# A float32 attention and FFN kernel: sign pass of the float64 weights on ScalarE, first products of two chunks interleaved, first tiles transposed by a diagonal

## The chip, the cores and the metric

The kernel runs on one core of one Trainium2 chip. The metric is the device time of one execution in microseconds (us). Before the change it took 611.33 us, the median of three runs (608.84 to 612.02).

## The reference

Four batches of 768 tokens with 8 heads of 64 go through a banded attention; each token then goes through a normalization and a two-layer network, whose weights are float64.

```
scores = scale * q @ k.T            # q, k, v: (4, 8, 768, 64) float32
keep = is_global | is_local         # first 8 keys, or 0 <= row - col < 96
scores = where(keep, scores - slope_h * dist, -1e9)
a = exp(scores - max(scores)); a = a / (sum(a) + 1e-9)
x = (a @ v) as (4, 768, 512)
xn = (x - mean(x)) / sqrt(var(x) + 1e-6) * g_ln
out = x + maximum(xn @ w_ch1, 0) @ w_ch2      # w_ch1 (512, 2048), w_ch2 (2048, 512), float64
```

## The kernel before

The 3072 tokens are 24 tiles of 128 rows; a chunk is two tiles (256 tokens), so there are twelve chunks. The first four tiles (t = 0 to 3, `TILES`) are the first 128 rows of each batch, for which one block of keys is enough; the program calls them `short`. They make up chunks 0 and 1. Their way is (names as in the trace): k and q are loaded (kf, qf) and transposed on TensorE (tk, tq), copied out of PSUM (kT, qT), multiplied to scores (s, two groups g of four heads). VectorE adds the mask and takes the negative maximum nm (T <- s, mask). ScalarE adds a constant to nm (mn) and takes the exponentials of each head with their sum (T <- T, mn). T is transposed on TensorE (tp), copied out (pT) and multiplied with v (pv). `divide` (L723) makes the reciprocal r of the sums and x = pv * r. Mean and variance follow, GpSimd raises to the power -0.5 (rs), `centred` writes (x - mean) * g into xs, `scaled` (L757) multiplies xs by rs, and `turn` (L450) transposes it on TensorE (tx). Two passes write it to xT as a sum of two f16 halves: high on ScalarE, low on VectorE. For the later tiles the transposes are DMAs, and their f16 low parts (pn, kn, xn, ul) are subtractions on GpSimd or VectorE.

All the big products are made of f16 halves. The weights are read as raw float64 and turned into an upper and a lower f16 by integer and float passes on 16 pieces of 128x1024 words (`weight`, L331 to 385). Pieces 0 to 7 are w1 (two per quarter of its columns, so steps 0 and 2 need pieces 0 and 1, steps 4 and 6 pieces 2 and 3, and so on), pieces 8 to 15 are w2. The passes of a piece n are, by their task names: wb, the load (1 MB); wr, `below` on ScalarE (bits below the mantissa); ws, `signs` on VectorE; wz, `sizes` on ScalarE (the float32 exponent rebased, absolute value); ww, `whole` on VectorE (shift and or); wu, the upper f16 (a cast, on whichever engine is chosen); wl, the lower f16 (a subtraction). In the trace the tile that they work on is st, or w2h or w2l where a piece has its home in the place of later weights. The sign pass before is

```
vec.tensor_scalar(out=halves[n][:, :, 1], in0=halves[n][:, :, 3],
                  scalar1=0x8000, scalar2=None, op0=ALU.bitwise_and)
```

A first product F{c}_{f} (`ffn1`, L809; f1_c_f in the order, f in the trace) takes xT of chunk c times two column blocks of w1: 24 matmuls of 128x256. Its result is evacuated as h in two f16 halves: a ReLU on ScalarE or VectorE, and a SCALAR_TENSOR_TENSOR on VectorE. The second products G (`ffn2`, L907) take h times w2. From the fifth chunk on, a scheme with seven products in place of eight takes over (R, uh, ul, m). None of this is touched by the change.

The order of the work comes from a planner (class `Plan`, L92 to 186). Each step is a task with an engine (or several, with a cost each), a cost in us, a rank, its predecessors and the buffers that it takes. A list scheduler gives each engine the task that can begin first; among those that can begin at about the same time, the lowest rank. A task with several engines goes to the one on which it would end first, with a handicap (`FAVOR` early, `LATER` later). The tables at the top (QUICK for the first tiles, PIECE and START for the weights) set the ranks. Gaps that the plan finds on TensorE before 90 us (`UNTIL`) are filled with `blank`, a product of the identity with itself (L264). Every instruction is issued through a helper (`Lane`), so all carry the line L204 in the trace. The first products are put in order by the loop at L1063 to 1090: all eight steps of chunk 0, then all eight of chunk 1, each after the one before it (`steps[-1:]`).

Of the kernel before, what the change touches and what calls it, by code (L numbers as in the profile page):

```python
# [24 lines left out]
P = 128  # L25
# [18 lines left out]
CT = 2  # L44
# [6 lines left out]

QUICK = (0.0, -5.2, 7.7, 16.9)
PIECE = (1.8, 5.3, 15.0)
START = 37.6
SIDE = (-1.1, 1.1)
UNTIL = 90.0


# [21 lines left out]
EVEN = 4  # L80
EARLY = 150.0
LEAD = 11
VRANK = 6.0
VLATE = 0.0
WEIGH = (-0.8, 0.2)
FAVOR = {"ACT": SIDE[0], "POOL": SIDE[1]}
# [103 lines left out]
def banded(ctx, tc, q, k, v, n_global, n_local, g_ln, w1, w2, out, flag):  # L190
# [37 lines left out]
    plan.room.update(ld=6, h=17, T=3, pn=3, pT=3, s=3, s1=1, pv=1, f1=2, f2=2, kT=3, vn=3, kT0=2, vn0=2, qT=2, r=2, tile=2, x=5, xT=2, st=3)  # L228
    task = plan.task
# [91 lines left out]
    for h in range(H):  # L321
        task(f"mask1_{h}", {"POOL": 0.87, "ACT": 0.42, "DVE": 0.3}, 0, lambda engine, h=h: build_mask1(h, engine), ["globals"], rank=45, port=True)
    task("gb", "SP", 0.6, lambda: load.dma_start(out=gb, in_=g_ln.partition_broadcast(P)), rank=9, dma=0.7)
# [7 lines left out]
    def weight(n):  # L331
# [50 lines left out]
        task(f"wl{n}", {"POOL": 2.2, "DVE": 1.24}, 0, lower, [f"wu{n}"], rank=rank, port=True)  # L382

# [65 lines left out]

    def turn(src, name, tag):  # L450
        ps = ps_f.tile([P, 4, P], F32, tag=tag, name=name)
        last = None
        for u in range(4):
            last = chain(last, pe.transpose(ps[:, u, :], src[:, u * P:(u + 1) * P], ident))
        return ps
# [131 lines left out]
    def tile_(t, ranks, gates):  # L587
# [116 lines left out]
        for g in range(ng_):  # L704
# [4 lines left out]
            task(f"R{t}_{g}", "DVE", 0.85 if short else 0.95, lambda g=g: reduce(g), [f"S{t}_{g}"] + ([f"mask0_{h}" for h in heads(g)] if short else []), rank=rank - 3, take={"T": [f"tp{t}_{g}" if short else f"pl{t}_{g}"]})  # L709
            task(f"E{t}_{g}", "ACT", 1.7 if short else 1.5, lambda g=g: exps(g), [f"R{t}_{g}"], rank=rank - 3)  # L710
            if short:
# [11 lines left out]
    def normal(t, rank, last, short):  # L723

        def divide():
            x, _, _ = place_x(t)
            sm = smalls[t][2]
            if short:
                r = p2.tile([P, H], F32, name="r")
                vec.tensor_scalar(out=r, in0=sm, scalar1=PS * 1e-9, scalar2=1.0 if short else VS, op0=ALU.add, op1=ALU.mult)  # L730
            else:
                r = made.pop(("r", t))
            vec.reciprocal(out=r, in_=r)
            vec.tensor_tensor(out=x, in0=sums.pop(t), in1=r.unsqueeze(2).to_broadcast([P, H, D]), op=ALU.mult)

        def divisor():
            made["r", t] = p2.tile([P, H], F32, name="r")
            act.activation(out=made["r", t], in_=smalls[t][2], func=AF.Copy, scale=VS, bias=PS * 1e-9 * VS)

# [69 lines left out]
    def ffn1(c, f, rank):  # L809
# [97 lines left out]
    def ffn2(ts, f, n, tags, rank):  # L907
# [152 lines left out]
    def due(step):  # L1060
        return START + step * place_rank

    for t in range(2 * CT):  # L1063
        tile_(t, [QUICK[t]] * 2, [[], []])
    for c in range(NC):
        if c < 2:
            for f in range(0, NF, 2):
                ffn1(c, f, due(len(steps)))
            if c == 0:
                continue  # L1070
# [294 lines left out]
```

## Time and profile before

| | before |
|---|---|
| median of three runs | 611.33 us (608.84 to 612.02) |
| profiled execution | 610.96 us, its span 609.2 us |
| TensorE (PE) busy | 590.0 us, 97% |
| TensorE weight loads (PEld) | 487.8 us, 80% |
| VectorE (DVE) busy | 518.7 us, 85% |
| ScalarE (ACT) busy | 410.5 us, 67% |
| GpSimd (POOL) busy | 160.5 us, 26% |
| granted clock of TensorE | 0.99 and more in every slice |

The page divides the span into 40 slices of 15.2 us. PE is at 8 or 9 tenths from the first slice, but until 90 us that includes the blanks. DVE is at 9 tenths through most of the first third. The wait lists put the idle time of an engine down to what ended it; a matmul's end is modelled, so starts are better than durations on PE.

### The profile page before, as it was taken

How to read it: one execution, taken by the hardware profiler on the slowest of the kernel's cores; microseconds unless marked ns; L12 is line 12 of the kernel's file. 1: busy time of each engine (PE TensorE's matmuls, PEld its weight loads, DVE VectorE, ACT ScalarE, POOL GpSimd, SP SyncE). 2: the span in 40 equal slices, each digit the busy share in tenths (PEclk: the TensorE clock that was granted, in tenths of full speed). 3: DMA queues.
4: the chain of work that ended last, by engine and by line, in shares of the span. 5: the costliest groups of instructions: out<-in, count | busy, mean ns of one | idle time of the engine just before them, and what ended most of it. 6: DMA issues, size and time to landing. Idle time of an engine off the chain costs nothing.

```text
span 609.2 us, 15299 instructions
## 1 busy us (share of the span) xinstructions
PE 590.0 (97%) x5913; PEld 487.8 (80%) x5913; DVE 518.7 (85%) x1248; ACT 410.5 (67%) x1008; POOL 160.5 (26%) x128
## 2 busy tenths in 40 slices
PE   8979899999999999999999999999999999999996
PEld 4757696556965885789999999999999999988885
DVE  5999999999999988899789899898898788484654
ACT  5988797875677866778676666889866755333330
POOL 2210112405464227252032032152232031040100
PEclk9999999999999999999999999999999999999999
DMA  8992989987988996985949866878966625100000
GB/s 220 304 320 97 226 204 199 231 195 126 222 165 184 198 168 138 185 172 112 168 122 132 148 156 110 156 153 148 165 140 98 130 53 88 36 36 18 36 2 37
DMA packets 247307, 88.33 MB, mean 145 GB/s; under 512 B 237376, under 2 KB 237376, under 8 KB 247232
## 3 DMA queue, kind: packets, MB, share of 16 engines
q1 hardware_dynamic: 246944, 87.32, 68.6%
q8 instruction: 47, 0.77, 0.5%
q14 instruction: 28, 0.23, 0.1%
q10 hardware_dynamic: 288, 0.00, 0.0%
HBM read 38.01 MB, written 6.29 MB: 73 GB/s over the span
## 4 chain that ended last, share of the span: by engine, by line
PE 62%; DVE 4%; DMA 2%; issue 1%; ACT 0%; SPq 0%; DVEq 0%
PE f L204 31%; PE m L204 24%; PE s L204 4%; PE pv L204 3%; DMA out_dram<-x 1%; DMA qT<-qT 1%; DMA xT<-xn 1%; DVE x L204 1%; DVE pn L204 0%; DVE T L204 0%; DVE w2l L204 0%; DVE R L204 0%; DVE vn L204 0%; DVE qn L204 0%; DVE xn L204 0%
## 5 line engine op out<-in xcount | busy, mean ns | idle before, releaser
L204 PE MATMUL f<-xT,w1h 128*128 128x256 f16 x1536 | 256.5, 273 | 7.8 <-DVE h L204 3.2
L204 PE MATMUL f<-xT,w1l 128*128 128x256 f16 x768 | 209.3, 273 | 0.0
L204 PEld LDWEIGHTS <-w1h 128*128 128x128 f16 x1536 | 147.4, 98 | 25.2 <-DVE xT L204 2.5
L204 DVE SCALAR_TENSOR_TENSOR R<-f,R 128x128 f32<-128x128 f32 x256 | 68.3, 288 | 35.0 <-ACT R L204 29.7
L204 ACT ACTIVATE T<-T,mn 128x256 f32<-128x256 f32 (+1 forms) x192 | 92.5, 482 | 3.5
L204 PEld LDWEIGHTS <-uh 128*128 128x128 f16 x896 | 85.9, 98 | 9.4
L204 PEld LDWEIGHTS <-w1l 128*128 128x128 f16 x768 | 75.1, 98 | 9.5 <-issue 0.8
L204 PE MATMUL f<-w2h,h 128*128 128x512 f16 x256 | 80.4, 379 | 0.5 <-DVE h L204 0.5
L204 ACT ACTIVATE uh<-R 128x896 f16<-128x896 f32 x57 | 53.9, 946 | 39.1 <-DVE R L204 39.0
L204 DVE CUSTOM_DVE_ANT_0 T<-s,mask 128x256 f32<-128x256 f32 (+1 forms) x192 | 68.2, 396 | 11.0 <-PE s L204 10.9
L204 ACT ACTIVATE R<-f 128x512 f32<-128x512 f32 x59 | 35.0, 594 | 62.6 <-PE f L204 61.1
L204 PE MATMUL m<-w2h,uh 128*128 128x256 f16 x256 | 69.8, 273 | 0.0
L204 PE MATMUL m<-w2l,uh 128*128 128x256 f16 x256 | 69.8, 273 | 0.0
L204 PE MATMUL m<-w2h,ul 128*128 128x256 f16 x256 | 69.8, 273 | 0.0
L204 PE MATMUL m<-t,uh 128*128 128x256 f16 x384 | 69.5, 273 | 0.0
L204 PEld LDWEIGHTS <-h 128*128 128x128 f16 x384 | 36.3, 98 | 40.1 <-issue 0.8
L204 POOL TENSOR_TENSOR ul<-R,uh 128x896 f16<-128x896 f32 x17 | 32.4, 1905 | 121.4 <-ACT uh L204 121.4
L204 DVE TENSOR_TENSOR ul<-R,uh 128x896 f16<-128x896 f32 x47 | 54.1, 1150 | 12.1 <-ACT uh L204 11.8
L204 POOL TENSOR_TENSOR pn<-T,pn 128x512 f16<-128x512 f32 x27 | 33.7, 1249 | 113.8 <-ACT pn L204 90.8
L204 PE MATMUL s<-kT,qT 128*128 128x128 f16 (+1 forms) x704 | 55.7, 225 | 2.0 <-ACT T L204 1.1
L204 PE MATMUL m<-t,ul 128*128 128x256 f16 x192 | 52.3, 273 | 0.0
L204 ACT ACTIVATE pn<-T 128x512 f16<-128x512 f32 x78 | 48.6, 623 | 2.3 <-DMA xT<-xn 0.9
(154 smaller groups left out, 1007.4 us busy)
## 6 DMA issues: line engine op xcount, KB each, us to landing
st<-in_moe_w_ch_dram SPq DMA_DIRECT2D x10, 1024.0 KB, 6.4
kf<-in_k_dram SPq DMA_DIRECT2D x28, 256.0 KB, 3.8
vf<-in_v_dram SPq DMA_DIRECT2D x28, 256.0 KB, 3.9
qf<-in_q_dram SPq DMA_DIRECT2D x24, 256.0 KB, 3.7
out_dram<-x SPq DMA_DIRECT2D x24, 256.0 KB, 2.6
qT<-qT SPq DMA_DIRECT2D x40, 128.0 KB, 2.6
w2h<-in_moe_w_ch_dram SPq DMA_DIRECT2D x3, 1024.0 KB, 7.7
w2l<-in_moe_w_ch_dram SPq DMA_DIRECT2D x3, 1024.0 KB, 9.6
```

The lines of the kernel that those rows point to most:

```text
L204: ins = getattr(self.engine, name)(*args, **kw)
```

## The change

It has five parts. (1) The sign pass may run on ScalarE too: there it reads the upper 32-bit word of the float64 as a float32, multiplies it by 2^-100 and writes an f16, which is a zero with the word's sign. (2) For the four first tiles the scaling of xs by rs is gone; instead the identity times rs (a 128x128 diagonal) is the right-hand operand of a float32 product that transposes xs and scales it at once. (3) The constant is no longer added to nm for these tiles; the divisor r takes an adjusted constant and is made on ScalarE. (4) The steps F of chunks 0 and 1 are put in order by MIX, and each waits for the step before it of its own chunk only. (5) All rank tables and several costs have new numbers, so the planner writes another order.

```
-QUICK = (0.0, -5.2, 7.7, 16.9)
-PIECE = (1.8, 5.3, 15.0)
-START = 37.6
+QUICK = (0.0, -57.0, 17.4, 26.0)
+PIECE = (24.7, 9.6, 9.5)
+START = 54.9
...
+MIX = [(0, n) for n in range(4)] + [(c, n + 4 * (1 - c)) for n in range(4) for c in (1, 0)] + [(1, n) for n in range(4, 8)]
...
-        def signs():
+        def signs(engine):
+            if engine == "ACT":
+                act.activation(out=halves[n][:, :, 1].bitcast(F16), in_=staged[n][1].bitcast(F32), func=AF.Copy, scale=2.0 ** -100)
+                return
             vec.tensor_scalar(out=halves[n][:, :, 1], in0=halves[n][:, :, 3], scalar1=0x8000, scalar2=None, op0=ALU.bitwise_and)
...
-        task(f"ws{n}", "DVE", 0.7, signs, [f"wr{n}"], rank=rank, port=True)
+        task(f"ws{n}", {"ACT": 1.24, "DVE": 1.34}, 0, signs, [f"wr{n}"], rank=rank, port=True)
...
-    def turn(src, name, tag):
+    def turn(src, name, tag, by=None):
...
+            if by is not None:
+                last = chain(last, pe.matmul(ps[:, u, :], lhsT=src[:, u * P:(u + 1) * P], rhs=by, start=True, stop=True))
+            else:
+                last = chain(last, pe.transpose(ps[:, u, :], src[:, u * P:(u + 1) * P], ident))
...
-            act.activation(out=mn[:, gsl], in_=nm[:, gsl], func=AF.Copy, bias=LN_PS)
+            if short:
+                mn = nm
+            else:
+                gsl = slice(g * gh, (g + 1) * gh)
+                act.activation(out=mn[:, gsl], in_=nm[:, gsl], func=AF.Copy, bias=LN_PS)
...
-        def scaled(engine):
-            xc = made["xc", t]
-            copy(engine, xc, xc, made["rs", t])
+        def diagonal(engine):
+            if engine == "ACT":
+                act.activation(out=made["diag"][t % 3], in_=ident, func=AF.Copy, scale=made["rs", t])
+            else:
+                vec.tensor_scalar(out=made["diag"][t % 3], in0=ident, scalar1=made["rs", t], scalar2=None, op0=ALU.mult)
...
-            made["xt", t] = turn(made["xc", t], f"tx{t}", "f1" if t < 2 else "f2")
+            made["xt", t] = turn(made["xc", t], f"tx{t}", "f1" if t < 2 else "f2", made["diag"][t % 3])
...
-        after = [...] + steps[-1:]
+        after = [...] + ([f"F{c}_{f - 2}"] * (f > 0) if c < 2 else steps[-1:])
```

The first place is ScalarE ahead of the last copy into xT0, which holds chunk 0 for its first product (T is a tile of exponentials, w2l the home of weight pieces 2 and 3 at that time; "less" marks the pass `below`, "big" the pass `sizes`, and w2l<-w2l alone is a sign pass). Before:

```order
L204 ACTIVATE xs0_424<-xs0_424,rs_359 128x512
L204 ACTIVATE xs1_407<-xs1_407,rs_397 128x512
L204 ACTIVATE mn_417<-nm_416 128x4
L204 ACTIVATE T2_0_434,sm_418<-T2_0_434,mn_417 128x128 x4
L204 ACTIVATE xT0_333<-tx1_460 128x4x128
L204 ACTIVATE xT0_333<-tx0_449 128x4x128
```

And now:

```order
L207 ACTIVATE T3_1_494,sm_442<-T3_1_494,nm_440 128x128 x4
L207 ACTIVATE r_519<-sm_442 128x8
L207 ACTIVATE xT1_424<-tx2_508 128x4x128
L207 ACTIVATE pT3_0_526<-tp3_0_514 128x512
L207 ACTIVATE w2l_86<-w2l_86,less_93 128x1024
L207 ACTIVATE pT3_1_549<-tp3_1_534 128x512
L207 ACTIVATE w2l_86<-w2l_86 128x1024
L207 ACTIVATE w2l_86,big_92<-w2l_86 128x1024
L207 ACTIVATE w2l_86<-w2l_86,less_93 128x1024
L207 ACTIVATE xT0_309<-tx0_562 128x4x128
```

The scalings of xs and the additions (mn) are gone; the exponentials of the last first tile, two weight pieces' passes and a copy into xT1 now stand ahead of the copy that fills xT0.

The second place is VectorE between the evacuations of the first products (h0_2 is step 2 of chunk 0, h1_0 step 0 of chunk 1; st4 to st6 are weight pieces). Before:

```order
L204 SCALAR_TENSOR_TENSOR st5_382<-st5_382 128x1024
L204 TENSOR_SCALAR st6_465<-st6_465 128x1024
L204 TENSOR_TENSOR xT1_589<-tx2_666,xT1_589 128x4x128
L204 SCALAR_TENSOR_TENSOR h0_2_615<-f1_0_2_564,h0_2_615 128x512
L204 TENSOR_TENSOR w1l_84<-st5_382,w1h_83 128x2x512
L204 TENSOR_SCALAR w2h_85<-w2h_85 128x1024
L204 SCALAR_TENSOR_TENSOR st6_465<-st6_465 128x1024
L204 SCALAR_TENSOR_TENSOR h0_4_741<-f1_0_4_629,h0_4_741 128x512
```

And now:

```order
L207 SCALAR_TENSOR_TENSOR h0_2_664<-f1_0_2_634,h0_2_664 128x512
L207 SCALAR_TENSOR_TENSOR st5_420<-st5_420 128x1024
L207 CAST w1h_83<-st5_420 128x2x512
L207 TENSOR_TENSOR w1l_84<-st5_420,w1h_83 128x2x512
L207 SCALAR_TENSOR_TENSOR st6_457<-st6_457 128x1024
L207 CAST w1h_83<-st6_457 128x2x512
L207 SCALAR_TENSOR_TENSOR h0_4_758<-f1_0_4_699,h0_4_758 128x512
L207 TENSOR_TENSOR w1l_84<-st6_457,w1h_83 128x2x512
L207 SCALAR_TENSOR_TENSOR h1_0_727<-f1_1_0_669,h1_0_727 128x512
L207 SCALAR_TENSOR_TENSOR h1_2_790<-f1_1_2_733,h1_2_790 128x512
```

The sign passes (TENSOR_SCALAR) have left this queue, the casts have come to it, and evacuations of chunk 1 stand between those of chunk 0.

## Rows read from the trace of the kernel before

**Rows 1.** Windows: stretch, us, busy (xinstructions) of PE PEld DVE ACT POOL, PEclk, DMA share, GB/s

```profile
0.00:39.00 39.00, 31.87 (x193) 20.83 (x193) 30.44 (x98) 30.80 (x88) 10.20 (x15) 1.00 0.90 269
39.00:70.00 31.00, 27.00 (x227) 22.53 (x228) 30.17 (x54) 25.21 (x50) 3.83 (x3) 1.00 0.64 200
70.00:100.00 30.00, 29.85 (x304) 26.60 (x303) 29.15 (x50) 27.22 (x56) 3.08 (x2) 1.00 0.92 199
100.00:250.00 150.00, 148.43 (x1361) 98.59 (x1360) 143.39 (x291) 106.30 (x281) 61.54 (x48) 1.00 0.92 182
```

**Rows 2.** PE's waits, 0 to 76 us: waited for, us in total, times, longest

```profile
PE f L204 <- DVE h L204: 3.2, 3, 1.9
PE f L204 <- ACT kT L204: 2.2, 1, 2.2
PE tx L204 <- ACT xs L204: 1.6, 1, 1.6
```

**Rows 3.** Timeline of PE: start, us, instruction, count, idle before and its releaser

```profile
39.24 0.28 PE L204 MATMUL f<-xT,w1h 128*128 128x256 f16 x1 [2.16 <-ACT kT L204]
...
69.92 0.38 PE L204 MATMUL f<-xT,w1h 128*128 128x256 f16 x2
...
72.54 0.60 PE L204 MATMUL tx<-ident,xs 128*128 128x128 f32 x4
72.97 0.38 PE L204 MATMUL f<-xT,w1h 128*128 128x256 f16 x2
```

**Rows 4.** Groups by form, weight passes: count, busy us, mean ns, idle before

```profile
L204 DVE TENSOR_SCALAR st<-st 128x1024 uint16<-128x1024 uint16 x10 | 13.0, 1346 | 0.0
L204 ACT ACTIVATE st<-st 128x1024 f32<-128x1024 f32 x10 | 11.5, 1147 | 0.2 <-DVE st L204 0.2
...
L204 ACT ACTIVATE w1h<-st 128x1024 f16<-128x1024 f32 x2 | 2.3, 1167 | 0.1
...
L204 DVE CAST w1h<-st 128x1024 f16<-128x1024 f32 x1 | 0.7, 686 | 0.0
```

**Rows 5.** Timeline of DVE up to the first product

```profile
10.15 0.29 DVE L204 CUSTOM_DVE_ANT_0 T<-s,mask 128x128 f32<-128x128 f32 x1 [1.12 <-PE s L204]
...
10.37 0.29 DVE L204 CUSTOM_DVE_ANT_0 T<-s,mask 128x128 f32<-128x128 f32 x1
...
20.68 1.23 DVE L204 TENSOR_TENSOR w1l<-w2h,w1h 128x1024 f16<-128x1024 f32 x1
21.82 0.17 DVE L204 TENSOR_SCALAR r<-sm 128x8 f32<-128x8 f32 x1
22.02 0.20 DVE L204 RECIPROCAL r<-r 128x8 f32<-128x8 f32 x1
...
24.08 1.35 DVE L204 TENSOR_SCALAR w2h<-w2h 128x1024 uint16<-128x1024 uint16 x1
25.21 1.40 DVE L204 TENSOR_SCALAR w2l<-w2l 128x1024 uint16<-128x1024 uint16 x1
...
38.51 1.28 DVE L204 TENSOR_TENSOR xT<-tx,xT 128x512 f16<-128x512 f32 x2
```

**Rows 6.** Timeline of ACT, one group of four exponentials

```profile
12.19 0.40 ACT L204 ACTIVATE T<-T,mn 128x128 f32<-128x128 f32 x1
...
13.74 0.57 ACT L204 ACTIVATE kT<-tk 128x512 f32<-128x512 f32 x1
```

**Rows 7.** Groups by form, the first tiles

```profile
L204 PE MATMUL s<-kT,qT 64*128 64x128 f32 x64 | 6.8, 284 | 1.5 <-ACT T L204 1.1 <-ACT qT L204 0.3
...
L204 ACT ACTIVATE xs<-xs,rs 128x512 f32<-128x512 f32 x4 | 2.8, 718 | 1.8 <-DVE xs L204 1.8
...
L204 ACT ACTIVATE mn<-nm 128x4 f32<-128x4 f32 x8 | 1.6, 195 | 0.0
```

**Rows 8.** Groups by form, low parts on POOL

```profile
L204 POOL TENSOR_TENSOR pn<-T,pn 128x512 f16<-128x512 f32 x27 | 33.7, 1249 | 113.8 <-ACT pn L204 90.8 <-DVE nm L204 12.1 <-issue 3.7
L204 POOL TENSOR_TENSOR ul<-R,uh 128x896 f16<-128x896 f32 x17 | 32.4, 1905 | 121.4 <-ACT uh L204 121.4
```

More of the change, by code (lines that the diff above doesn't have):

```diff
@@ L80 @@
 EVEN = 4
[L81 to L85, printed above, removed]
+EARLY = 153.0
+LEAD = 9
+VRANK = 14.4
+VLATE = 15.0
+WEIGH = (-1.4, -0.21)
 FAVOR = {"ACT": SIDE[0], "POOL": SIDE[1]}
@@ L227, in banded @@
     plan = Plan()
-    plan.room.update(ld=6, h=17, T=3, pn=3, pT=3, s=3, s1=1, pv=1, f1=2, f2=2, kT=3, vn=3, kT0=2, vn0=2, qT=2, r=2, tile=2, x=5, xT=2, st=3)
+    plan.room.update(ld=6, h=17, T=3, pn=3, pT=3, s=3, s1=1, pv=1, f1=2, f2=2, kT=3, vn=3, kT0=2, vn0=2, qT=2, r=2, tile=2, x=5, xT=2, st=3, dg=3)
     task = plan.task
@@ L262, in starts, with beside @@
         pool.memset(made["ones"], 1.0)
+    def beside():
+        made["aside"] = aside = p2.tile([P, 1024], F16, tag="pn", name="aside", bufs=3)
+        made["diag"] = [aside[:, 2 * P * n:2 * P * (n + 1)].bitcast(F32) for n in range(3)]
     def blank():
@@ L312, in banded @@
     task("ident", "DVE", 0.3, lambda: vec.tensor_scalar(out=ident, in0=made["rel"][:, 1, :], scalar1=0.0, scalar2=None, op0=ALU.is_equal), ["starts"])
+    task("beside", "DVE", 0.0, beside, ["ident"], rank=-4, take={"pn": [f"xt{2 * CT - 1}"]})
     task("asked", "ACT", 0.95, asked, rank=-50, dma=-4.7)
@@ L321, in banded @@
     for h in range(H):
-        task(f"mask1_{h}", {"POOL": 0.87, "ACT": 0.42, "DVE": 0.3}, 0, lambda engine, h=h: build_mask1(h, engine), ["globals"], rank=45, port=True)
+        task(f"mask1_{h}", {"POOL": 1.4, "ACT": 0.42, "DVE": 0.3}, 0, lambda engine, h=h: build_mask1(h, engine), ["globals"], rank=45, port=True)
     task("gb", "SP", 0.6, lambda: load.dma_start(out=gb, in_=g_ln.partition_broadcast(P)), rank=9, dma=0.7)
@@ L374, in weight @@
         rank = PIECE[0] + PIECE[1] * n if n < 8 else START + 2.62 * (16 + 2 * (n - 8)) - PIECE[2]
+        rank += SHIFT[n]
         before = {7: ["wl0"], 8: ["wl2"]}.get(n, [])
@@ L381, in weight @@
         task(f"wu{n}", {"ACT": 1.17, "POOL": 1.95, "DVE": 0.75}, 0, upper, [f"ww{n}"] + (["wl1"] if n == 8 else []) + (["wl3"] if n in (8, 9, 10, 11) else []) + (["wl7", "wl8"] if n >= 12 else []), rank=rank, port=True)
-        task(f"wl{n}", {"POOL": 2.2, "DVE": 1.24}, 0, lower, [f"wu{n}"], rank=rank, port=True)
+        task(f"wl{n}", {"POOL": 2.42, "DVE": 1.24}, 0, lower, [f"wu{n}"], rank=rank, port=True)
     for n in range(NF):
@@ L709, in tile_ @@
             task(f"R{t}_{g}", "DVE", 0.85 if short else 0.95, lambda g=g: reduce(g), [f"S{t}_{g}"] + ([f"mask0_{h}" for h in heads(g)] if short else []), rank=rank - 3, take={"T": [f"tp{t}_{g}" if short else f"pl{t}_{g}"]})
-            task(f"E{t}_{g}", "ACT", 1.7 if short else 1.5, lambda g=g: exps(g), [f"R{t}_{g}"], rank=rank - 3)
+            task(f"E{t}_{g}", "ACT", 1.5, lambda g=g: exps(g), [f"R{t}_{g}"], rank=rank - 3)
             if short:
@@ L727, in divide @@
             sm = smalls[t][2]
[L728 to L732, printed above, removed]
+            r = made.pop(("r", t))
             vec.reciprocal(out=r, in_=r)
@@ L737, in divisor @@
             made["r", t] = p2.tile([P, H], F32, name="r")
-            act.activation(out=made["r", t], in_=smalls[t][2], func=AF.Copy, scale=VS, bias=PS * 1e-9 * VS)
+            act.activation(out=made["r", t], in_=smalls[t][2], func=AF.Copy, scale=1.0 if short else VS, bias=1e-9 if short else PS * 1e-9 * VS)
         def stats():
@@ L784, in normal @@
         c, n_ = divmod(t, CT)
-        if not short:
-            task(f"Z{t}", "ACT", 0.2, divisor, [f"E{t}_3"], rank=rank - 4, take={"r": [f"X{t}"]})
-        task(f"X{t}", "DVE", 1.1 if short else 0.92, divide, [last] + ([] if short else [f"Z{t}"]), rank=rank - 4, take={"h" if t == 2 * CT + 1 else "x": [f"O{t}"]})
+        task(f"Z{t}", "ACT", 0.2, divisor, [f"E{t}_0", f"E{t}_1" if short else f"E{t}_3"], rank=rank - 4, take={"r": [f"X{t}"]})
+        task(f"X{t}", "DVE", 0.92, divide, [last, f"Z{t}"], rank=rank - 4, take={"h" if t == 2 * CT + 1 else "x": [f"O{t}"]})
         task(f"B{t}", "DVE", 0.72, stats, [f"X{t}"], rank=rank - 4)
         task(f"A{t}", "DVE", 0.3, spread, [f"B{t}"], rank=rank - 4)
-        task(f"W{t}", "POOL", 0.98, root, [f"A{t}"], rank=rank - 12)
+        task(f"W{t}", "POOL", 0.6, root, [f"A{t}"], rank=rank - 12)
         task(f"C{t}", "DVE", 0.74, centred, [f"A{t}", "gb"], rank=rank - 4, take={"T": [f"xt{t}" if short else f"xl{t}"]}, port=True)
@@ L793, in normal @@
         if short:
-            task(f"xr{t}", {"ACT": 0.75, "DVE": 0.7}, 0, scaled, [f"W{t}", f"C{t}"], rank=rank - 4)
-            task(f"xt{t}", "PE", 0.7, flip, [f"xr{t}"], rank=rank - 20, take={"f1" if t < 2 else "f2": [f"xl{t}"]}, slack=1.0 * (t > 1))
+            task(f"xr{t}", {"ACT": 0.3, "DVE": 0.25}, 0, diagonal, [f"W{t}", "beside"], rank=rank - 4, take={"dg": [f"xt{t}"]}, port=True)
+            task(f"xt{t}", "PE", 0.9, flip, [f"xr{t}", f"C{t}"], rank=rank - 20, take={"f1" if t < 2 else "f2": [f"xl{t}"]}, slack=1.0 * (t > 1))
             task(f"xh{t}", "ACT", 0.66, turned_high, [f"xt{t}"], rank=rank - 4, take=whole)
@@ L866, in ffn1 @@
         j = f // 4
-        after = [f"{'xa' if c > 1 else 'xl'}{t}" for t in range(CT * c, CT * c + CT)] + [f"wl{2 * j}", f"wl{2 * j + 1}"] + steps[-1:]
+        after = [f"{'xa' if c > 1 else 'xl'}{t}" for t in range(CT * c, CT * c + CT)] + [f"wl{2 * j}", f"wl{2 * j + 1}"] + ([f"F{c}_{f - 2}"] * (f > 0) if c < 2 else steps[-1:])
         if c < 2:
@@ L918, in ffn2 @@
         cs = sorted({t // CT for t in ts})
-        after = [f"hl{c}_{f_}" for c in cs for f_ in range(f, f + n, 2)] + [f"wl{(NF + f_) // 2}" for f_ in range(f, f + n, 2)] + steps[-1:]
+        after = [f"hl{c}_{f_}" for c in cs for f_ in range(f, f + n, 2)] + [f"wl{(NF + f_) // 2}" for f_ in range(f, f + n, 2)] + (["F0_14", "F1_14"] if c == 0 and f == 0 else steps[-1:])
         take = {}
@@ L1063, in banded @@
     for t in range(2 * CT):
-        tile_(t, [QUICK[t]] * 2, [[], []])
+        tile_(t, [QUICK[t] + GROUP[2 * t], QUICK[t] + GROUP[2 * t + 1]], [[], []])
     for c in range(NC):
[L1066 to L1070, printed above, removed]
+        if c == 0:
+            continue
+        if c == 1:
+            for c_, n in MIX:
+                ffn1(c_, 2 * n, due(len(steps)))
             for f in range(0, NF, 2):
```

6 lines of the change are left out of this document (3 added, 3 removed).

## The prediction

> **What bounds the kernel now.** I read the windows first. From 70 us on TensorE hardly stops: in 70 to 100 us PE is busy for 29.85 of 30.00 us [rows 1], and the list of PE's waits from 70 to 600 us adds up to no more than 3.3 us. The lever is therefore ahead of 70 us. In 0 to 39 us PE's 31.87 us are swollen by blanks (products of the identity with itself that fill planned gaps, 71 records in all), and in 39 to 70 us it still lacks 4 us. The second view, PE's waits up to 76 us, says for whom it waits: 3.2 us for DVE's evacuation of a first product (h), 2.2 us for ACT in front of the first of them, 1.6 us for the scaled tile xs [rows 2]. DVE explains all three: 30.44 of 39.00 us although it has next to nothing to do before 6 us, then 30.17 of 31.00 us, while ACT has 25.21 of 31.00 us and POOL 3.83 [rows 1]. So what sets the end is the time at which PE begins to run without gaps; DVE's queue, and after it ACT's, sets that.
>
> The anchors are in PE's timeline [rows 3]. The first product of chunk 0 starts at 39.24 us. From 69.92 us on PE runs on, with two steps of chunk 0 and eight of chunk 1 ahead of it. A step is 24 records: 72.54 - 69.92 = 2.62 us. A turn of four transposes takes 72.97 - 72.54 = 0.43 us.
>
> **The change, part by part.** *Sign.* By the order, 15 of the 16 sign passes leave DVE for ACT. The profile has all 16 on DVE, ten of them on the tile st at 1.35 us each [rows 4]; between starts it is 25.21 - 24.08 = 1.13 us [rows 5], so DVE loses 15 x 1.13 = 17 us. No row shows the new form on ACT, a strided float32 read with an f16 write. Its bounds are the pass on the same words (1.147 us) and the f16 cast (1.167 us) [rows 4], less the overlap of some 0.1; from below I keep 1.0, from above twice the row, 2.3, since a write to every fourth half-word is in no row. I take 1.13, by the nearest row. In return seven more uppers of pieces are DVE's: 7 x 0.65 = 4.6 us by the cast of 0.686 us [rows 4].
>
> The Trainium skill, page "ScalarE: Activation LUTs", section "Rules for kernel authors", speaks against this move: simple operations belong on VectorE, up to about three times as fast per element. The rows above do not show that for this strided pass, 1.35 on DVE against 1.15 on ACT; by the rule the sign would be 3.4 us on ACT, and the sum is that of the slower rival below.
>
> *Small passes.* Four scalings of a 128x512 tile (0.718 us on ACT) become diagonals of 128x128, for which I take 0.3 us, between 0.2 and 0.4 (one exponential of 128x128 takes 0.40 [rows 6]). Eight additions of a constant (0.195 us each) go [rows 7]. The divisor's 0.2 us goes from DVE to ACT.
>
> *Turning by a diagonal.* The transposes become float32 products. The rows record such a product as two: 64 records of s for 32 products [rows 7]. At 0.43 / 4 = 0.107 us a record, four products take 0.86 us where four transposes take 0.43. Bounds are 0.43 (no change) and 1.7. Three of the four turns lie in PE's waiting before its first step; the fourth costs 0.43 us.
>
> The Trainium skill, page "TensorE: Matmul & The Clock Gate", section "Terms", gives the transpose mode as four times as fast for float32. By that a turn would take 4 x 0.43 = 1.7 us and the fourth turn 1.3 us; the time would come out 0.9 us later. The two recorded passes of s speak for a factor of two.
>
> *Order.* All four first tiles now come before the first step, and the steps run 0, 0, 1, 0, 1, 0, 1, 1 (chunk numbers), so that the second half of the w1 pieces is wanted only by the ninth step. The first step therefore starts later than 39.24 us, and the question is whether PE then runs on. Two queues decide when it starts, S.
>
> DVE, from the first reduction to the last subtraction into xT0, new order (durations between starts of the same form, means of the lines view where no row is named): 32 reductions x 0.21 [rows 5] = 6.7; seven masks x 0.31 and a small one 2.4; two copies of q and one of p 1.8; one sign 1.1; four chains from reciprocal to rs, 24.08 - 22.02 = 2.06 each [rows 5], 8.2; four centred tiles x 0.66 = 2.6; words, cast and lower of pieces 0 and 1, (1.13 + 0.65 + 1.14) x 2 = 5.8 (the lower is 21.82 - 20.68 [rows 5]); three subtractions x 0.6 = 1.8; a diagonal 0.2. Sum 30.7 us. The same count over the old order gives 27.3 us, and the trace took 39.79 - 10.15 = 29.64 us for it [rows 5], 8% more, for waits. The new stretch starts about 0.4 us later (a copy of q and a fifth mask now lie ahead of it): 10.55 + 30.7 x 1.08 = 43.7 us.
>
> ACT, from the first exponentials to the last copy into xT0: eight groups x (13.74 - 12.19) = 12.4 [rows 6]; nine weight passes x 1.13 = 10.2; 13 copies out of PSUM x 0.5 = 6.5; divisors and diagonals 1.1. Sum 30.2 us from about 11.5: 41.7 us without waits, and DVE's last subtraction comes after it. Both queues say the same: S is 42.3 us with no wait at all, 44 us with the waits of before. I take 44.
>
> From S on PE needs 16 x 2.62 + 0.86 + 0.43 (two blanks) to the end of chunk 1; before, from 69.92 us, it needed 10 x 2.62 + 0.43. The four groups of scores among them are the same. Gain = 69.92 + 26.2 + 0.43 - (S + 41.9 + 1.3) = 53.3 - S = 9.3 us.
>
> Does PE keep running? From the first evacuation to that of step 14 of chunk 0, 11 steps later, PE needs 11 x 2.62 + 1.3 = 30.1 us. In the new order DVE has 27.6 us of work there by the same durations (29.8 with 8% of waits), ACT 28.0 us (30.2). That is even, with no cover left: one wait on either is PE's. I take off 1 us. Blanks fall from 71 to 44 records, which is free, for they stand in planned gaps; the granted clock is 1.00 in every window [rows 1] with waits of up to 2.2 us in it [rows 2], so I expect no fall of it.
>
> *Later.* 27 low parts of pn and 11 of ul go from DVE to POOL, at 1.249 and 1.905 us [rows 8], which adds some 55 us to POOL's 160. DVE is busy for 143.39 of 150 us in 100 to 250 us [rows 1], so PE can only stay ahead there because this work leaves. I cost it at nothing: what hides it is the distance between the lower part and its use. Of the few waits after 70 us I keep all. From the last chunk's first step on every engine has the order it had.
>
> Sum: 9.3 - 1.0 = 8.3 us. The profiled execution took 610.96 us (span 609.2), the median of three runs is 611.33, 0.4 above it; so 603.0 us against the median. Half a per cent, 3.1 us, is about what a measurement of this kernel can tell from no change.
>
> **The rivals.** *The start slips* (chance 0.17). S is a chain through four engines, and the loads of the last first tile come after seven others and two weight pieces: DMA's share is 0.90 in 0 to 39 us [rows 1]. Were S 49 to 52 us, the gain is 53.3 - S, less 1: 0 to 3 us, 608 to 611. For it: the new order makes ACT as full as DVE. Against it: both queues reach 42 by work alone, and 8% was all that the old one lost.
>
> *Given back in the middle* (0.08). With PE 8 us earlier, low parts on POOL (twice DVE's time) and ACT's additional 11 us make some chunk's xT late; 3 to 5 us come back: 606 to 608. Against it: DVE's work ahead of the seventh tile's result is 15 us less by the same count.
>
> *More* (0.09). S at 42.3, and the 3.3 us of waits after 70 us go as well, for DVE is eased: 611.3 - 12 = 599.
>
> *Slower: the sign pass is dear on ACT* (0.06). Its place is ACT's queue from 23 to 75 us, with nine such passes ahead of the last evacuation of chunk 0. ACT has a lead of 30.1 - 28.0 = 2.1 us there. With an excess e per pass PE loses 9 x e - 2.1: at e = 1.15, a pass of 2.3 us, the gain of 8.3 is gone, and above 2.7 us the kernel is clearly slower; at three times the row, 3.4 us, it is 603 + 9 x 2.27 - 2.1 = 621 us. Against it: the two rows of ACT on the same words agree within 2%.
>
> **How the numbers follow.** The forecast, S from 42 to 47 us, has 0.60 and the time 603.0. The range goes to the rival with more gain below and to S = 51 above: 599 to 609; outside lie the slower case, part of the slipping start and a little below. Faster by over 0.5% are the forecast, the case with more, most of the middle case and half of the slipping start: 0.82. Same: 0.11. Slower: 0.07.
>
> **What would show it.** Right: the first product of chunk 0 starts between 42 and 47 us; the last step of chunk 1 ends near 90 us where it was 99; the wait for DVE h up to 76 us falls below 1.5 us; ACT has 15 sign passes of about 1.15 us; a turn by the diagonal takes 0.86 us. Wrong: a start after 49 us, waits of PE for ACT between the steps, a sign pass over 1.5 us, a clock below 1.00, or new waits for xT or for T between 100 and 300 us that eat what the front has won.

## The result and the profile after

The changed kernel took 617.22 us, the median of four executions (612.68 to 620.7), where the kernel before took 611.2 (four executions). The ratio is 1.0107, with a 95% interval of 1.006 to 1.0155: slower by about 1%. The forecast was 603.0. The profiled execution took 612.68 us, its span 610.9.

First the windows, the same stretches and columns as [rows 1].

```profile
0.00:39.00 39.00, 34.32 (x231) 25.77 (x232) 29.87 (x119) 31.68 (x99) 4.43 (x14) 1.00 0.93 291
39.00:70.00 31.00, 27.98 (x237) 23.28 (x237) 23.56 (x32) 30.81 (x30) 1.16 (x2) 1.00 0.46 145
70.00:100.00 30.00, 26.78 (x227) 21.77 (x225) 25.72 (x41) 29.82 (x43) 3.57 (x2) 0.94 0.78 183
100.00:250.00 150.00, 146.25 (x1332) 96.87 (x1331) 129.21 (x276) 113.08 (x281) 71.01 (x58) 0.99 0.86 178
```

DVE is relieved, as meant: 23.56 of 31.00 us in the second stretch, where it had 30.17. ACT has taken its place, with 30.81 of 31.00 and then 29.82 of 30.00 us. PE has less time busy than before in 70 to 100 and in 100 to 250 us, and its granted clock falls.

The groups by form give the price. These rows answer to [rows 4]; the last two are new.

```profile
L207 ACT ACTIVATE st<-st 128x1024 f16<-128x1024 f32 x10 | 25.1, 2507 | 0.1
...
L207 ACT ACTIVATE st<-st 128x1024 f32<-128x1024 f32 x10 | 11.4, 1142 | 0.2
...
L207 PE MATMUL tx<-aside,xs 128*128 128x128 f32 x32 | 4.4, 282 | 0.1
...
L207 ACT ACTIVATE aside<-ident,rs 128x128 f32<-128x128 f32 x2 | 0.8, 388 | 0.0
```

The sign pass (f32 read, f16 written) takes 2.507 us, the pass on the same words with a float32 result 1.142. Fifteen of them are on ACT (ten on st, five on w2h and w2l).

PE's timeline, as [rows 3], and the waits. The list of waits is for 0 to 80 us and, after the dots, for 80 us to the end.

```profile
39.81 1.11 PE L207 MATMUL tx<-aside,xs 128*128 128x128 f32 x8
40.76 2.75 PE L207 MATMUL blank<-ident 128*128 128x512 f16 x12
44.05 0.27 PE L207 MATMUL f<-xT,w1h 128*128 128x256 f16 x1 [0.55 <-ACT xT L207]
...
76.96 0.38 PE L207 MATMUL f<-xT,w1h 128*128 128x256 f16 x2 [2.05 <-DVE h L207]
...
95.24 0.38 PE L207 MATMUL f<-w2h,h 128*128 128x512 f16 x1
...
142.60 0.38 PE L207 MATMUL f<-w2l,h 128*128 128x512 f16 x1 [2.93 <-DVE w2l L207]
```

```profile
PE f L207 <- DVE h L207: 2.8, 2, 2.0
PE f L207 <- ACT xT L207: 1.4, 2, 0.8
...
PE f L207 <- DVE w2l L207: 2.9, 1, 2.9
PE s L207 <- DVE kT L207: 1.7, 2, 0.9
```

The first product starts at 44.05 us; the forecast had 44. The number is right, but not the queue behind it. The forecast had DVE's last subtraction into xT0 as the last step, with ACT done by 41.7 us. Here it is ACT's copy that comes last, and DVE waits 1.55 us for it (the first line is ACT's, the second DVE's):

```profile
43.44 0.57 ACT L207 ACTIVATE xT<-tx 128x512 f16<-128x512 f32 x1
...
44.04 0.69 DVE L207 TENSOR_TENSOR xT<-tx,xT 128x512 f16<-128x512 f32 x1 [1.55 <-ACT xT L207]
```

What follows is not as forecast. The wait "for DVE h" at 76.96 us is ACT's in truth. DVE's timeline and ACT's show the order:

```profile
76.22 0.69 DVE L207 SCALAR_TENSOR_TENSOR h<-f,h 128x512 f16<-128x512 f32 x1 [1.34 <-ACT h L207]
```

```profile
70.60 1.26 ACT L207 ACTIVATE w2l<-w2l,less 128x1024 int32<-128x1024 uint32 x1
71.75 1.15 ACT L207 ACTIVATE w1h<-w2h 128x1024 f16<-128x1024 f32 x1
72.78 0.59 ACT L207 ACTIVATE h<-f 128x512 f16<-128x512 f32 x1
73.26 2.50 ACT L207 ACTIVATE w2l<-w2l 128x1024 f16<-128x1024 f32 x1
75.49 0.69 ACT L207 ACTIVATE h<-f 128x512 f16<-128x512 f32 x1
```

ACT runs without a gap; a sign pass of 2.50 us stands ahead of an evacuation, DVE's half of the same evacuation waits 1.34 us for ACT's, and PE 2.05 us for DVE. In the chain of waits of 44 to 100 us the passes of ACT on st, w2l and w2h hold 62% (40.5, 14.9 and 6.7); these are all of ACT's passes on a piece, of which the sign is the longest.

At 142.60 us PE waits for the low part of the last weight piece. In the kernel before it was done at 131.3 us, in the changed one at 142.5. The pieces of w2 go through the same queue of ACT, where the upper half of this piece begins at 136.0 us. The rest of the delay is DVE's, which comes to the subtraction at 140.53 us, behind another tile's normalization, and takes 2.01 us for it.

Four anchors from the timelines of PE and DVE tell where the time went (us; "cut sign" is a run below):

| | before | changed | cut sign |
|---|---|---|---|
| first product of chunk 0 | 39.2 | 44.1 | 45.7 |
| first second product (f<-w2h) | 99.4 | 95.2 | 89.9 |
| first R of the fifth chunk | 254.3 | 256.7 | 245.3 |
| end of PE | 604.4 | 606.0 | 594.7 |

At 95 us the changed kernel is still 4.1 us ahead, where the forecast had 9. Between there and the fifth chunk it loses 6.5: the waits for h at 98 us (1.2), for w2l (2.9) and kT (1.7), and a lower clock.

The clock's fall stands in the windows of 5 us behind the two longest waits (columns as in [rows 1]):

```profile
75.00:80.00 5.00, 3.04 (x20) 2.39 (x20) 3.75 (x7) 5.00 (x9) 0.00 (x0) 0.82 0.69 100
80.00:85.00 5.00, 5.00 (x41) 4.19 (x39) 3.90 (x6) 4.97 (x5) 0.00 (x0) 0.84 0.93 227
140.00:145.00 5.00, 2.40 (x7) 0.90 (x7) 5.00 (x11) 3.23 (x9) 3.48 (x3) 0.80 0.17 40
145.00:150.00 5.00, 5.00 (x31) 2.49 (x30) 4.30 (x10) 4.09 (x13) 2.59 (x2) 0.85 0.78 169
```

In the kernel before all four are at 1.00. PE's timeline shows the lower of the clock's two levels, 1.2 in place of 2.4 GHz: from 78.3 to 81.5 us a first product's record takes 0.21 us where it took 0.11, and from 143.0 to 146.4 us a record of 128x512 takes 0.43 where it took 0.21. By the four windows the falls cost some 3.4 us of this execution, (0.18 + 0.16 + 0.20 + 0.15) x 5; that is an estimate.

The four executions of the changed kernel had mean clocks of 0.994, 0.997, 0.983 and 0.981, at 612.7, 614.6, 619.9 and 620.7 us. Between the first and the slowest, 0.013 of 611 us is 7.9 us, and the times differ by 8.0. But the clock is not all of it: the second has the highest clock and is 1.9 us longer than the first.

### The profile page after: what moved, and what is told of

Read it like the earlier page. It is cut to its first block, busy times and chain, and to the rows that moved or that the text cites. A ratio compares the mean times of both kernels' runs of the same rounds, so it can differ in the third digit from the quotient of the medians.

```text
span 610.9 us, 15316 instructions
## 1 busy us (share of the span) xinstructions
PE 590.5 (97%) x5902; PEld 488.9 (80%) x5902; DVE 477.4 (78%) x1190; ACT 436.9 (72%) x1012; POOL 218.5 (36%) x174
## 4 chain that ended last, share of the span: by engine, by line
PE 77%; ACT 15%; DVE 4%; DMA 1%; issue 1%; POOL 0%; POOLq 0%
PE f L207 42%; PE m L207 24%; PE s L207 6%; ACT st L207 5%; PE pv L207 4%; ACT w2l L207 2%; ACT T L207 2%; ACT w2h L207 2%; DMA pT<-pn 1%; ACT h L207 1%; DVE st L207 1%; DVE h L207 1%; PE blank L207 1%; DVE T L207 1%; ACT pT L207 1%
## 5 line engine op out<-in xcount | busy, mean ns | idle before, releaser
L207 POOL TENSOR_TENSOR pn<-T,pn 128x512 f16<-128x512 f32 x54 | 68.8, 1274 | 108.0 <-ACT pn L207 52.0
L207 PE MATMUL f<-w2h,h 128*128 128x512 f16 x256 | 82.0, 384 | 1.2 <-DVE h L207 1.2
L207 ACT ACTIVATE T<-T,mn 128x256 f32<-128x256 f32 x160 | 80.0, 501 | 4.1 <-ACT mn L207 0.4
L207 POOL TENSOR_TENSOR ul<-R,uh 128x896 f16<-128x896 f32 x28 | 54.1, 1933 | 75.8 <-ACT uh L207 71.0
L207 ACT ACTIVATE R<-f 128x512 f32<-128x512 f32 x64 | 37.9, 592 | 60.3 <-PE f L207 58.1
L207 ACT ACTIVATE uh<-R 128x896 f16<-128x896 f32 x64 | 60.4, 943 | 26.0 <-DVE R L207 25.8
L207 PE MATMUL s<-kT,qT 128*128 128x128 f16 (+1 forms) x704 | 57.0, 225 | 1.9 <-DVE kT L207 1.7
L207 DVE TENSOR_TENSOR ul<-R,uh 128x896 f16<-128x896 f32 x36 | 41.1, 1143 | 17.1 <-ACT uh L207 17.0
L207 PE MATMUL f<-w2l,h 128*128 128x512 f16 x128 | 49.3, 385 | 2.9 <-DVE w2l L207 2.9
```

What stands on the lines that cost most here:

```text
L207: ins = getattr(self.engine, name)(*args, **kw)
```

## The experiments

Each median is compared with the kernel before on the same chip (609.6 to 610.6 us).

**1. Sign back on DVE, order kept.** In `signs` the branch for ACT is taken out.

```
-            if engine == "ACT":
-                act.activation(out=halves[n][:, :, 1].bitcast(F16), ...)
-                return
```

> The changed kernel with its order kept, but all 16 sign passes issued on DVE (at the place in the program where the plan put them on ACT). Theory A (the price of the sign pass on ACT, 2.5 us in the trace where the forecast had 1.13): ACT loses 15 x 2.24 = 34 us, about 13 of them between 45 and 75 us, where it was at 100%; DVE gets 15 x 1.13 = 17 us. The waits of PE between 44 and 100 us (5.5 us) and the one for w2l at 143 us go, the granted clock stays at 0.998 or more, and the time is 603 to 606 us, that is 5 to 9 us below the kernel before. Theory B (the new order of steps or the late start costs the time, whoever makes the sign): 611 us or more, with PE waits between 50 and 80 us as in the changed kernel.

Measured: 612.82 us, ratio 1.0042 (1.0021 to 1.0063). It is 4.4 us below the changed kernel's median, but theory A's 603 to 606 was missed, and the time lies where theory B had it (611 or more). The windows show another reading than B's: DVE is full again.

```profile
39.00:70.00 31.00, 28.02 (x238) 23.54 (x238) 30.47 (x39) 19.46 (x28) 1.91 (x2) 1.00 0.46 147
70.00:100.00 30.00, 26.42 (x225) 21.17 (x224) 28.78 (x44) 21.18 (x37) 3.70 (x2) 0.94 0.93 205
```

ACT has 19.46 of 31.00 us, DVE 30.47, and PE waits for h for 5.2 us up to 100 us. Giving the 17 us back to DVE takes away what the order was made for. So this run could not tell whether the order is sound.

**2. Measured prices in the planner's table,** `{"ACT": 2.25, "DVE": 1.14}` for the sign pass, everything else of the change as it is.

> The changed kernel, with the sign pass at 2.25 us on ACT and 1.14 on DVE in the planner's table (it had 1.24 and 1.34), so that the planner makes its choice and its whole order with prices from the trace. Theory A: most signs go to DVE; 603 to 608 us, clock 0.998 or more. Theory B: no better than 611. A third reading (the ranks were made for the old prices and fit nothing else): between 608 and 613, with new waits ahead of 100 us.

Measured: 616.88 us, ratio 1.0109 (1.0083 to 1.0136). Theory A missed, in its reason too: ten of the sixteen signs are still on ACT. The time is one that theory B allows (no better than 611) and above the range of the third reading, whose sense the waits bear out. PE waits 2.1 us for one qT at 23 us, and behind 100 us 2.5 for w2l, 2.2 for kT and 2.0 for x. Prices alone, with ranks made for others, gained nothing.

**3. The old order, sign on ACT.** In the kernel before, `signs` gets the changed kernel's form for n > 0.

> The kernel before with its order kept, and the sign passes of pieces 1 to 15 issued on ACT in place of DVE; nothing else changed. Theory A: a pass of 2.5 us there too; ACT was busy for 25.2 of 31.0 us between 39 and 70 us and gets some 6 x 2.24 = 13.4 us in that stretch, 7 to 8 us more than there is room, and as much pressure ahead of 39 us: 617 to 628 us, granted clock below 0.998. Theory B (the pass is harmless, the new order is what costs): 609 to 612 us.

Measured: 636.1 us, ratio 1.0416 (1.039 to 1.0441). The pass takes 2.479 us there.

```profile
L204 ACT ACTIVATE st<-st 128x1024 f16<-128x1024 f32 x10 | 24.8, 2479 | 0.0
```

Theory A holds in its direction, and the loss, 26 us, is larger than it had. DVE sinks to 20.82 of 31.00 us in 39 to 70 us, and PE waits 7.0 us for one qT of ACT and 6.8 us for h.

**4. What in the pass is dear.** Six passes on ACT ahead of the last piece's sign, such as

```
+                act.activation(out=to[:, ::2], in_=hi[:, 0], func=AF.Copy, scale=small)
+                act.activation(out=lo16[:, :512], in_=gb, func=AF.Copy, scale=small)
```

> The changed kernel with six additional passes on ACT ahead of the sign pass of the last weight piece, to price the form of the write. Five read 512 float32 values and one 256: (1) strided read to 512 contiguous f16; (2) to f16 at every second place; (3) to f16 at every fourth place, as the sign does; (4) the same as bf16; (5) contiguous read, f16 at every fourth place; (6) the same with 256. If a two-byte write at a stride is what costs: (1) about 0.60 us, (3), (4) and (5) 1.3 to 1.4, (6) 0.75, and (2) tells whether the stride of 4 bytes costs it as well. If it is the read together with the write: (5) about 0.6. If it is the f16 type: (4) about 0.6. The time of the kernel itself tells nothing here; some 6 us of ACT are added.

ACT's timeline has the first two (contiguous f16, then every second place), the groups the others.

```profile
133.33 0.66 ACT L207 ACTIVATE w2h<-st 128x512 f16<-128x512 f32 x1
...
134.02 0.79 ACT L207 ACTIVATE w2h<-st 128x512 f16<-128x512 f32 x1
```

```profile
L207 ACT ACTIVATE st<-gb 128x512 f16<-128x512 f32 x1 | 1.3, 1346 | 0.0
L207 ACT ACTIVATE st<-st 128x512 bf16<-128x512 f32 x1 | 1.3, 1342 | 0.0
L207 ACT ACTIVATE st<-st 128x512 f16<-128x512 f32 x1 | 1.3, 1336 | 0.0
L207 ACT ACTIVATE st<-gb 128x256 f16<-128x256 f32 x1 | 0.8, 773 | 0.0
```

It is the write of two bytes at every fourth half-word: 1.34 us for 512 elements, with f16 as with bf16, from a contiguous source as from a strided one. At every second place it is 0.79 us, contiguous 0.66. An element costs (1346 - 773) / 256 = 2.24 ns.

**5. The waits filled.** Nine blanks ahead of step 12 of chunk 0, twelve products with zeros ahead of the second product that waits for w2l.

```
+            for _ in range(9 if (c, f) == (0, 12) else 0):
+                blank()
...
+                for _ in range(12 if (t, f) == (2, 14) else 0):
+                    pe.matmul(sums2[t], lhsT=ident.bitcast(F16)[:, :P], rhs=fill.bitcast(F16)[:, :1].to_broadcast([P, DM]), start=False, stop=False)
```

> The changed kernel with its two longest waits of PE filled: nine blanks ahead of step 12 of chunk 0 (the wait of 2.0 us at 77 us) and twelve products with zeros, which add nothing to the sum, ahead of the second product that waits 2.9 us for the last weight piece at 142 us. No wait is made shorter by it. Theory clock (the granted clock falls behind a long wait of PE, and that is what the slower executions have more of): the windows 75 to 85 and 140 to 150 us, 0.82 and 0.85 in the changed kernel, go to 1.00; the profiled execution, 612.7, falls by 3 us to some 609.5, and the median, 617.2, by 4 to 7, to 610 to 613. Rival (the clock follows something else): as the changed kernel, 613 to 621, with a clock of 0.98 to 0.997.

Measured: 616.1 us, ratio 1.0082 (1.0053 to 1.0111). The windows at the filled places are at 1.00, as the theory of the clock had it. The time is the rival's (613 to 621): the clock fell elsewhere, behind a wait of 2.0 us for pT at 28.7 us and one of 2.9 us for h at 102 us.

```profile
30.00:35.00 5.00, 5.00 (x26) 4.47 (x26) 3.19 (x8) 4.43 (x17) 0.99 (x1) 0.50 1.03 420
35.00:40.00 5.00, 5.00 (x28) 4.02 (x26) 4.68 (x20) 3.23 (x16) 0.00 (x0) 0.63 1.02 408
75.00:80.00 5.00, 5.00 (x46) 4.31 (x45) 4.59 (x6) 5.00 (x7) 0.00 (x0) 1.00 1.04 300
...
100.00:105.00 5.00, 2.13 (x9) 0.88 (x9) 4.62 (x9) 4.89 (x12) 0.45 (x1) 0.86 1.05 261
```

So the falls stand behind waits. The wait for h has grown from 1.2 us, for ACT's queue is no shorter. The one for pT lies ahead of both filled places, so the edit did not bring it; the changed kernel's own execution waited 1.2 us there, and its clock did not fall. How much of the 617 us is the clock's and how much the waits' stays open.

**6. The sign pass at the price of the forecast.** The order of the changed kernel, and the pass cut to 416 of 1024 words; the sign of the other 608 is left out.

```
-                act.activation(out=halves[n][:, :, 1].bitcast(F16), in_=staged[n][1].bitcast(F32), ...)
+                act.activation(out=halves[n][:, :416, 1].bitcast(F16), in_=staged[n][1][:, :416].bitcast(F32), ...)
```

> The changed kernel, order kept, with the sign pass on ACT cut to the first 416 of 1024 words, so that it takes about the 1.13 us that the forecast gave it (0.2 + 416 x 2.24 ns by the probe); the other words lose their sign, that part of the computation is left out. Theory A (only the price of this pass was wrong in the forecast's sum): the first product at 43 to 44 us, the last first product of chunk 1 done by 91 us, 602 to 606 us. Theory C (the new order loses in the second products, 100 to 180 us, whatever the sign costs): the lead at 97 us is there, but PE waits for w2l between 130 and 145 us, and the time is 607 to 611.

Measured: 601.66 us, ratio 0.9873 (0.9832 to 0.9914). Theory A holds, theory C falls.

```profile
L207 ACT ACTIVATE st<-st 128x416 f16<-128x416 f32 x10 | 11.4, 1137 | 0.1
```

```profile
39.00:70.00 31.00, 31.00 (x266) 26.42 (x265) 28.20 (x41) 29.60 (x39) 1.84 (x2) 0.99 0.61 194
70.00:100.00 30.00, 29.32 (x253) 22.78 (x251) 25.81 (x49) 26.23 (x52) 3.37 (x2) 1.00 0.87 216
100.00:250.00 150.00, 148.94 (x1408) 102.28 (x1407) 134.07 (x287) 110.96 (x287) 77.86 (x64) 1.00 0.91 184
```

With a pass of 1.137 us PE has no gap from 39 to 70 us, the second products start at 89.9 us, and the wait for w2l is gone. (The first product came at 45.7 us, later than expected, behind a clock of 0.66 in 35 to 40 us.) One term, the length of this pass, separates 602 from 617. That the values left wrong change no time by themselves is taken for granted; no run tests it.

**7. The small parts alone,** in the old order: diagonals, float32 turns, no added constant.

> The kernel before with its order kept and only the small parts of the change: diagonals and float32 products in place of four scalings and transposes, no added constant for the first tiles; sign pass, steps and tables as before. By the prices of the forecast ACT gains 8 x 0.2 + 4 x 0.4 = 3 us ahead of 77 us, DVE nothing, PE loses 0.43 us a turn, most of it in waits: 608.5 to 610.5 us, about 0.5 us faster than before on the same chip. Rival (a product in place of a transpose is four times as dear, 1.3 us more a turn, or the diagonal is late): 611 or more.

Measured: 609.32 us, ratio 0.9981 (0.996 to 1.0001). That is the size expected, and it can't be told from no change. The diagonal takes 0.392 us on ACT.

**8. Ranks searched anew.** The table as in 2, and QUICK, PIECE, START, SHIFT, GROUP and the other rank tables found again by the length of the plan.

> The changed kernel with the sign pass at its measured prices in the planner's table (ACT 2.25, DVE 1.14 us), and ranks searched anew for these prices by the length of the plan alone. The plan's own length for it is no shorter than for the kernel before. Theory A (the change's gain in the plan came from a sign pass priced at 1.24 us on ACT; with the real price there is nothing to win by the rest): 607 to 614 us. Rival (the interleaving and the diagonals are worth several us by themselves, once the ranks fit): 606 or less.

Measured: 608.07 us, ratio 0.9959 (0.994 to 0.9979). Inside theory A's range, but its reason is too strong: with the real price there is something to win.

**9. Sign on POOL,** order kept.

```
+                pool.tensor_scalar(out=halves[n][:, :, 1].bitcast(F16), in0=staged[n][1].bitcast(F32), scalar1=2.0 ** -100, scalar2=None, op0=ALU.mult)
```

> The changed kernel, order kept, with the 15 sign passes that were on ACT issued on GpSimd (POOL) at the same places of the program, as a multiplication of the float32 by 2^-100 with an f16 result. POOL was busy for 1.2 of 31 us between 39 and 70 us, so it has room. Its price there is in no run; the f16 upper of a piece took 1.9 us on POOL in the kernel before. Theory A (all that the changed kernel lacks is room on ACT): about 2 us a pass, 602 to 607 us, the lead of the cut sign pass. Rival (the pass is as dear on POOL, 2.5 us or more, or the longer way of each piece makes weights late): PE waits for w1l or w2l, 608 us or more.

Measured: 634.14 us, ratio 1.0374 (1.0348 to 1.0399). The rival holds: the pass is dearest here.

```profile
L207 POOL TENSOR_SCALAR st<-st 128x1024 f16<-128x1024 f32 x10 | 45.6, 4559 | 32.3 <-ACT st L207 32.2
```

**10. A price between,** 720 of 1024 words, otherwise as 6.

> As the run with the cut sign pass, but with 720 of 1024 words: by the probe 0.2 + 720 x 2.24 ns = 1.8 us a pass (the other words lose their sign, that part is left out). If the loss follows the forecast's own rule for this rival, nothing until ACT's lead of 2.1 us is used up and then 9 passes times the excess, it is 9 x 0.67 - 2.1 = 3.9 us more than the forecast's case: 605 to 607 us. If it is in proportion to the excess (15.5 us for 1.37 us): 609 to 610 us. If the loss is a step (the clock falls or not): at 602 or at 615.

Measured: 605.1 us, ratio 0.9911 (0.989 to 0.9932), with a pass of 1.832 us. By the forecast's own rule for a dear pass it is 9 x (1.83 - 1.13) - 2.1 = 4.2 us above run 6, 605.9. A loss in proportion and a step are out. But the loss is not where the rule has it, in the first products (the pass, then PE's timeline):

```profile
L207 ACT ACTIVATE st<-st 128x720 f16<-128x720 f32 x10 | 18.3, 1832 | 0.1
...
89.07 0.38 PE L207 MATMUL f<-w2h,h 128*128 128x512 f16 x1
...
136.02 0.38 PE L207 MATMUL f<-w2l,h 128*128 128x512 f16 x1 [2.26 <-DVE w2l L207]
```

The second products start at 89.07 us, earlier than run 6's 89.86. Behind that, up to the first R of the fifth chunk (248.1 against 245.3 us), it loses 3.6 us, with the wait for w2l among it.

**11. The old order with the cut pass on ACT,** 416 of 1024 words, as 3 otherwise.

> The kernel before, order kept, with the sign passes of pieces 1 to 15 on ACT and cut to 416 of 1024 words (1.13 us a pass; the other words lose their sign, that part is left out). It tells what the move of the pass is worth without the new order. If moving a pass of 1.13 us from DVE to ACT is the gain by itself: 601 to 606 us. If the gain needs the interleaved steps (in the old order all of w1 is wanted by the eighth step, and the passes stand on ACT ahead of evacuations): 608 to 616 us.

Measured: 614.9 us, ratio 1.0077 (1.0051 to 1.0102). Even at 1.13 us the move alone loses some 4 us; with the new order around it the same pass wins 8.5. The gain needs both.

**12. A longer search** of the ranks of 8.

> As the run with the sign pass at its measured prices and ranks searched anew, after a longer search; its plan is 2.0 us shorter than that one's. If the plan's length carries over to the chip, 605 to 608 us, at least 0.4% faster than the kernel before; if the difference of two plans of this size is lost in waits that the plan does not know, 608 to 611.

Measured: 604.84 us, ratio 0.9914 (0.989 to 0.9939). Nothing is left out here, and it is faster than both kernels. The planner now puts seven sign passes on ACT and nine on DVE, and the load is even:

```profile
39.00:70.00 31.00, 30.11 (x238) 23.60 (x237) 29.86 (x44) 30.10 (x46) 1.84 (x2) 1.00 0.61 189
70.00:100.00 30.00, 29.89 (x275) 25.34 (x273) 26.13 (x44) 26.92 (x48) 3.45 (x2) 1.00 1.00 221
100.00:250.00 150.00, 149.89 (x1378) 101.29 (x1376) 128.12 (x273) 112.32 (x285) 78.26 (x64) 1.00 0.82 173
```

The first product starts only at 51.1 us, seven later than in the changed kernel, and the time is 12 us less: PE is busy for 149.89 of 150 us where the changed kernel had 146.25.

## Why the prediction was wrong

**The price of the sign pass** is the step that failed: "I take 1.13, by the nearest row". Two rows stood there, one with a float32 written at the same stride, one with an f16 written without a gap. They agreed within 2%, and that was taken for evidence; but the new form had what neither had, two bytes written at every fourth place. It measured 2.507 us (run 4 shows the write to be the cause), and with the forecast's price the same order takes 601.7 us, 8.5 less than the kernel before where 8.3 were forecast (run 6). The bound from above, 2.3 us, nearly held it, and the text named the write as its reason; the chances did not follow: 0.06 for a case that one unmeasured operation decides, fifteen times over.

**The rule of that rival** has the direction, but only part of the size, and not the place. PE loses 9 x e - 2.1. With e = 2.51 - 1.13 = 1.38 that is 10.3 us, and 603.0 + 10.3 = 613.3 where the median is 617.2. The profiled execution, 612.68, is near the rule's 610.96 - 8.3 + 10.3 = 613.0, but it is the fastest of the four, so that is luck in part. From run 6 to run 10 the median rises by 3.4 us where the rule has 4.2, and from run 10 to the changed kernel by 12.1 where it has 6.1. The rule puts all of it ahead of the last evacuation of chunk 0. By the anchors the changed kernel loses 5.4 us against run 6 up to the second products and 6.0 more from there to the fifth chunk. The waits for w2l and the falls of the clock were in no term of the sum.

**The start** was right in part by luck. The forecast's 43.7 us came from DVE, with 8% for waits. Two sign passes stand in ACT's queue ahead of the copy into xT0. Together they took some 2.5 us more than priced, and ACT's 41.7 us became 44.0 (43.44 + 0.57), which is close to what DVE had been given.

The sign takes 1.32 us on DVE in the changed kernel's one case, as an AND of uint16, and 2.5 on ACT, 1.9 times. The Trainium skill, page "ScalarE: Activation LUTs", section "Rules for kernel authors", wants simple operations on VectorE and gives up to about three times the speed for bf16 with one source; the prediction left that condition out. The trace agrees in the direction. Run 4 adds that the form of the write makes most of it.

**The other steps.** The turn by a diagonal: 0.95 us for eight records (40.76 - 39.81 in PE's timeline), where 0.86 was forecast and a turn by transposes took 0.43, a factor of 2.2. The Trainium skill, page "TensorE: Matmul & The Clock Gate", section "Terms", gives the transpose mode as four times as fast for float32, which would make it 1.7 us; the trace does not agree. The diagonals: 0.39 us on ACT and 0.28 on DVE, 0.3 forecast. The sum of small parts: run 7 is 0.9 us faster than the kernel before, about as expected, but within noise. Low parts on POOL at no cost: 54 of pn at 1.274 us and 28 of ul at 1.933, and no long wait of PE for either. (They are not "twice DVE's time": the kernel before has 1249 ns against 800 and 1905 against 1150, 1.6 and 1.7 times. And some of DVE's passes are longer in the changed kernel, vn 1092 ns where it was 849, xs 945 where it was 810; whether POOL's work is the reason no run shows.) The clock, "so I expect no fall of it": wrong; it was argued from a wait of 2.2 us in the old kernel that left the clock at 1.00 [rows 2], and here a wait of 2.05 us came with a fall to 0.82.

**What run 6 does not show** is a safe margin: "even, with no cover left" was right too. ACT had 29.60 of 31.00 us with the cheap pass.

## What to carry to other kernels

An operation of a new form is priced by what is new in it: element size and stride of the write and the engine, not the number of elements. If no row shows that, a range that holds both ends and a chance that follows it are worth more than the nearest row; how often the operation stands in the queue that will then be fullest tells how much hangs on it. And a plan made by costs has to be made again, ranks included, when a cost is corrected: the price alone gained nothing, price and ranks together 0.9%.

## What was not expected of the hardware

ACT writes two bytes at every fourth half-word at 2.24 ns an element, where 1024 float32 at the same stride take 1.142 us in all, 1.1 ns each. POOL takes 4.56 us for 1024 of the same, 3.5 times DVE's 1.32. In run 9 two low parts that DVE began 0.2 and 0.4 us behind the start of such a pass of POOL took 2.00 and 2.01 us; eight that it began 0.97 us or more into one took 1.21 to 1.25, as with POOL idle.

The length of a wait alone does not tell whether the clock falls. In run 6 waits of PE of 1.42 and 0.95 us (for pT, at 28 and 34 us) were followed by a granted clock of 0.66 in 35 to 40 us, in run 10 waits of 1.45 and 0.93 us for the same by 1.00 (run 6, then run 10; columns as in [rows 1]).

```profile
35.00:40.00 5.00, 5.00 (x29) 4.27 (x29) 4.69 (x13) 4.18 (x16) 0.49 (x1) 0.66 1.03 411
...
35.00:40.00 5.00, 4.74 (x39) 3.95 (x38) 4.61 (x10) 4.97 (x12) 0.92 (x1) 1.00 1.03 408
```

A late start of PE can be worth its time: run 12 starts 12 us after the kernel before and ends 5 us ahead of it.
